# Transposes of normalised tokens and attention outputs: from TensorE to the DMA engines

## The chip, the cores and the metric

The kernel runs on one core of a Trainium2 chip. The metric is the device time of one execution in microseconds (us), lower is better. The engines are PE (TensorE), DVE (VectorE), ACT (ScalarE), POOL (GpSimd) and SP (SyncE, which here only issues DMAs). In the traces PE's results lie in PSUM (`ps_all`), from where DVE or ACT copy them to the working memory, SBUF.

## The reference

Two layers, each of them attention followed by a gated MLP, on 2048 tokens of width 512, in bfloat16:

```python
def _A_ref(x, wq, wk, wv, wo):             # 32 heads of 16, one shared key and value
    q = heads(x @ wq); k = x @ wk; v = x @ wv
    p = softmax(einsum('bhqd,bkd->bhqk', q, k) * 16 ** -0.5)
    return merge(einsum('bhqk,bkd->bhqd', p, v)) @ wo

def _B_ref(x, w_in, w_sp, b_sp, w_out):    # F = 1792, halves of 896
    z = gelu(x @ w_in)
    z1, z2 = z[..., :896], layernorm(z[..., 896:])
    g = einsum('ts,bsf->btf', w_sp, z2) + b_sp[None, :, None]
    return (z1 * g) @ w_out

x = x + A(layernorm(x)); x = x + B(layernorm(x))     # layer 0
x = x + A(layernorm(x)); x = x + B(layernorm(x))     # layer 1, same weights
```

There are 32 heads x 2048 x 2048 exponentials per layer. A *block* below is 128 keys x 512 columns of scores; there are 4096 blocks in all.

## The kernel before

The kernel is written by a list scheduler in Python. Every operation has an engine, an assumed duration, dependencies and a priority; the scheduler plays them against a model of the core and emits one fixed instruction order per engine, with semaphore waits. So any edit of a duration in the model gives another order of the same work.

The exponential of a block is computed in one of two ways. ACT takes groups of two or three blocks with one `ACTIVATE`. DVE takes a pair of blocks now and then, with a polynomial of seven instructions. The scheduler decides block by block:

```python
    def take(self, t, js):                 # may DVE take a block, at time t?
        if sc.bank_free() > t:             # needs one of the two side banks of PSUM
            return None
        ...
            backlog = sc.free["dve"] - t + sum(o.dur for o in sc.ready["dve"] if ...)
            if backlog > BACKLOG:
                return None
```

Layer norm of token tiles (128 tokens x 512), then four PE transposes per tile into a side bank, and a copy out of PSUM by DVE, or by ACT if it has a gap:

```python
        def pe(e, b):
            ins = None
            for i, sl in enumerate(slots):
                for kd in range(KD):
                    k = i * KD + kd
                    ins = e.transpose(self.b16(b)[:, k * 128:(k + 1) * 128],
                                      self.xn[:, sl, kd * 128:(kd + 1) * 128], self.ident[:])
            return ins
        ...
        pt, (ev,) = sc.job([(pe, n * 4 * 0.06)], [dict(
            fn=lambda e, b: e.tensor_copy(*cp(b)), dur=d_psum(n * 256), prio=pr, deps=dst_deps,
            alts=[("act", lambda e, b: e.activation(*cp(b), ACTF.Copy), d_act(n * 512) + 0.1)])], ...)
```

`ln` serves the keys of a layer (destination `xnTA`) and the MLP's input (`xnTB`). `project` does the same for the attention output `on`, into `onT`, before the multiplication with `wo`. Tokens come in chunks of 512, 512, 512, 256, 128 and 128; the work of one chunk's MLP runs beside the next chunk's attention. When the last chunk's attention is over, a serial chain finishes the layer, and the second layer's keys can start.

The softmax here doesn't subtract the row's maximum and nothing guards it: scores larger than these inputs give would overflow.

Of the kernel before, what the change touches and what calls it, by code (L numbers as in the profile page):

```python
# [57 lines left out]
class Sched:  # L58
# [3 lines left out]
    def __init__(self, side_banks):  # L62
        self.free = {e: 0.0 for e in ENGS}
        self.ready = {e: [] for e in ENGS}
        self.streams = {e: [] for e in ENGS}
        self.order = {e: [] for e in ENGS}
        self.commits = []
        self.banks = [Bank(b) for b in side_banks]
        self.seq = 0
        self.table = "exp"  # L70
        self.cache = {}
        self.nleft = 0
        self.exp_next = None
        self.tick = {}
        self.hist = []
        self.lent = {}
        self.dma_free = 0.0

    def lend(self, key, idxs, o):
# [139 lines left out]
    def commit(self, o, t, eng=None):  # L219
        eng = eng or o.eng  # L220
        if eng != o.eng:
            for e, f, d in o.alts:
                if e == eng:
                    o.fn, o.dur = f, d
        if o.ready is not None:
            if o in self.ready[o.eng]:
                self.ready[o.eng].remove(o)
                self.cache.pop(o.eng, None)
            for e, _f, _d in o.alts:
                if o in self.ready[e]:  # L230
                    self.ready[e].remove(o)
                    self.cache.pop(e, None)
        o.eng = eng
        if o.first:
            b = min([b for b in self.banks if not b.busy and not b.closed], key=lambda b: b.free_at)
            b.busy = True
            o.job.bank = b
            o.deps += [d for d in b.rel if d not in o.deps]
        o.start = t
        dur = o.dur  # L240
        if eng == "pe":
            k = int(t / TICK)
            if not self.fast(t):
                dur = o.slow
            self.hist.append((t + dur, o.cols))
            k = int((t + dur) / TICK)
            self.tick[k] = self.tick.get(k, 0.0) + o.cols
        if o.table is not None and o.table != self.table:
            self.table = o.table
            dur += 1.3  # L250
        o.end = t + dur
        o.vis = o.end + (LAT[eng] if o.lat is None else o.lat)
        if o.dma:
            self.dma_free = max(self.dma_free, o.end) + o.dma / 240e3
            o.vis = self.dma_free + 1.9
        self.free[eng] = o.end
        self.order[eng].append(o)
        self.commits.append(o)
        self.nleft -= 1
        if o.job is not None and o in o.job.last:  # L260
            o.job.left -= 1
            if o.job.left == 0:
                b = o.job.bank
                b.busy = False
                b.rel = list(o.job.last)
                b.free_at = max(x.vis for x in o.job.last)
        self.cache.pop(eng, None)
        for u in o.users:
            u.nun -= 1
            if u.nun == 0:  # L270
                self._arm(u)
        if o.at_commit is not None:
            o.at_commit(o)
        return o
# [106 lines left out]
def d_act(n):  # L381
    return n * 0.8333e-3 + 0.06

# [22 lines left out]
class Kern:  # L406
    def __init__(self, nc, A_x, A_wq, A_wk, A_wv, A_wo, B_x, B_w_in, B_w_sp, B_b_sp, B_w_out, out):
# [42 lines left out]
        self.xn = sb([P, 4, D], BF16, "xn")  # L450
        self.xnTA = sb([P, KD, S], BF16, "xnTA")
        self.xnTB = sb([P, KD, 512], BF16, "xnTB")
        self.qs = sb([P, NQS, 512], BF16, "qs")
# [11 lines left out]
        self.on = sb([P, 4, D], BF16, "on")  # L465
        self.onT = sb([P, 4, 512], BF16, "onT")
        self.rden = sb([P, 2, 4, 4], FP32, "rden")
# [55 lines left out]
    def b16(self, b):  # L523
        return self.ps16[:, 1024 * b:1024 * (b + 1)]

    def dma(self, fn, deps, sem, nbytes, prio=5.0, eng="sp", issue=0.5):
# [77 lines left out]

    def ln(self, tiles, deps_t, dst, dst_deps, pr, urgent=False):
        sc = self.sc
# [15 lines left out]
        for t in tiles:  # L622
# [5 lines left out]
                op1=ALU.mult), 0.22, [r, self.last_xn[sl]], pr + 0.3))  # L628

        def pe(e, b):  # L630
            ins = None
# [7 lines left out]
        def cp(b):  # L639
            return (dst.rearrange("p kd (t c) -> p t kd c", c=128),  # L640
                    self.b16(b)[:, 0:n * 512].rearrange("p (t kd c) -> p t kd c", t=n, kd=KD))
        pt, (ev,) = sc.job([(pe, n * 4 * 0.06)], [dict(
            fn=lambda e, b: e.tensor_copy(*cp(b)), dur=d_psum(n * 256), prio=pr, deps=dst_deps,  # L643
            alts=[("act", lambda e, b: e.activation(*cp(b), ACTF.Copy), d_act(n * 512) + 0.1)])], xo + [self.c_id], pr)
        for sl in slots:
            self.last_xn[sl] = pt
        return ev


    def layer_keys(self, layer):  # L650
        sc = self.sc
        for p in range(8):
            def build(p=p):
# [4 lines left out]
                for tt in ([ts[:1], ts[1:]] if p < 2 else [ts]):  # L658
                    evs.append(self.ln(tt, lambda t: [self.x_op[t]],
                                       self.xnTA[:, :, tt[0] * 128:(tt[-1] + 1) * 128], dd, pr, p < 2))  # L660
                self.xnTA_read[p] = []

                def kpe(e, b):
                    ins = None
                    for kd in range(KD):
                        ins = e.matmul(self.b32(b)[:, 0:256], self.wk_rep[:, kd, :], self.xnTA[:, kd, p * 256:(p + 1) * 256],
                                       start=(kd == 0), stop=(kd == KD - 1))
                    return ins

                def vpe(e, b):  # L670
                    ins = None
                    for i, t in enumerate(ts):
                        for kd in range(KD):
                            ins = e.matmul(self.b32(b)[:, 256 + 128 * i:384 + 128 * i],
                                           self.xnTA[:, kd, t * 128:(t + 1) * 128], self.wv_rep[:, kd, :],
                                           start=(kd == 0), stop=(kd == KD - 1))
# [79 lines left out]
    def make_q(self, q, war=()):  # L756
# [4 lines left out]
        def pe(e, b, h):  # L761
            ins = None
            for i in range(g.nh):
                for kd in ((0, 1), (2, 3))[h] if g.nh == 1 else range(4):
                    if g.nh == 1 or i // (g.nh // 2) == h:
                        ins = e.matmul(self.b32(b)[:, i * n:(i + 1) * n], self.wq_pad[:, kd, g.hg + i, :],  # L766
                                       self.xnTA[:, kd, g.t0:g.t0 + n], start=(kd == 0), stop=(kd == KD - 1))
            return ins
# [63 lines left out]
    def project(self, g, norms):  # L832
# [7 lines left out]
        for h in range((nq + 1) // 2):  # L840
# [11 lines left out]
            def cp(b, qts=qts):  # L852
                m = len(qts)
                return (self.onT[:, :, qts[0] * 128:(qts[0] + m) * 128].rearrange("p c (qt q) -> p c qt q", q=128),
                        self.b16(b)[:, 0:m * 512].rearrange("p (qt c q) -> p c qt q", qt=m, c=4))
            m = len(qts)
            pl, (ev,) = sc.job([(pe, m * 4 * 0.06)], [dict(
                fn=lambda e, b, cp=cp: e.tensor_copy(*cp(b)), dur=d_psum(m * 256), prio=0.7, deps=list(self.onT_read),
# [6 lines left out]
        for qt in range(nq):  # L865
            t = g.t0 // 128 + qt

            def pe(e, b, qt=qt):
                ins = None
                for c in range(4):  # L870
                    ins = e.matmul(self.b32(b)[:, 0:D], self.onT[:, c, qt * 128:(qt + 1) * 128], self.wo_r[:, c, :],
                                   start=(c == 0), stop=(c == 3))
                return ins
            pl, (xo,) = sc.job([(pe, 4 * d_mm(512))], [dict(
                fn=lambda e, b, t=t: e.tensor_tensor(self.X[:, t, :], self.b32(b)[:, 0:D], self.X[:, t, :], ALU.add),
                dur=d_psum(512), prio=0.8, deps=[self.x_op[t]])], [evs[qt // 2], self.l_wo], 1.4)
            self.onT_read.append(pl)
# [4 lines left out]
    def mixer_chunk(self, g):  # L882
# [8 lines left out]
        for i in range(0, nt, 2):  # L891
            ts = T[i:i + 2]
            evs.append(self.ln(ts, lambda t: [self.x_op[t]], self.xnTB[:, :, i * 128:(i + len(ts)) * 128], war, pr, last))
        self.xnTB_read = []
        z2 = []
        z1 = []
        for i, t in enumerate(T):
            for h in range(2):
                def pe(e, b, ks, i=i, h=h):
                    ins = None  # L900
                    for kd in ks:
                        ins = e.matmul(self.b32(b)[:, 0:448], self.xnTB[:, kd, i * 128:(i + 1) * 128],  # L902
                                       self.w_in_r[:, kd, FH + h * 448:FH + (h + 1) * 448], start=(kd == 0),
# [3 lines left out]
                def cp(b, t=t, h=h):  # L907
# [8 lines left out]
                                                d_act(448) + 0.1)])],  # L916
                                   [evs[i // 2], self.l_win], pr + 0.2)
                z2.append(ev)
# [12 lines left out]
        for f0 in range(0, NF, per):  # L931
# [3 lines left out]
            def pe(e, b, part, f0=f0):  # L935
                ins = None
                for (f, kd) in part:
                    ins = e.matmul(self.b32(b)[:, (f - f0) * n:(f - f0 + 1) * n], self.w_in_r[:, kd, f * 128:(f + 1) * 128],  # L938
                                   self.xnTB[:, kd, 0:n], start=(kd == 0), stop=(kd == KD - 1))
                return ins  # L940
# [33 lines left out]
        else:  # L974
            gs = z1 = [sc.op("act", gl, d_act(NF * nt * 128) + d_act(nt * FH), z1 + z2, -1.0, table="gelu")] * (2 * nt)
        for (zt, zn, v) in zs:
# [116 lines left out]
    def closing(self, layer):  # L1093
# [9 lines left out]
        for tc in range(8):  # L1103
# [43 lines left out]
            for tt in range(2):  # L1147
                t = tc * 2 + tt

                def pe(e, b, ks, tt=tt, par=par):  # L1150
# [8 lines left out]
                    dur=d_psum(512), prio=0.8, deps=[self.x_op[t]])], [self.l_wout], pr - 0.3,  # L1159
                    piece_deps=[hs[0:1], hs[1:2], hs[2:4]], soft=evs)  # L1160
                self.hT_read[par].append(pl)
# [482 lines left out]
```

## Time and profile before

| | before |
|---|---|
| median of all runs (us) | 1877.7 when predicted, 1878.4 with one run more |
| span of the profiled run | 1873.8 us |
| busy: ACT, DVE, PE | 1764.5, 1745.3, 1609.1 us |
| blocks by ACT, by DVE | 3599, 497 |
| attention of layer 0 ends, of layer 1 ends | 885.78, 1819.05 us |

The page gives the busy time and share of the span for each engine:

```profile
span 1873.8 us, 30967 instructions
PE 1609.1 (86%) x12242; PEld 498.9 (27%) x12242; DVE 1745.3 (93%) x3131; ACT 1764.5 (94%) x1580; POOL 53.4 (3%) x94
```

The view by windows tells stretches apart. Columns: start and end, length, then busy us and instructions of PE, PEld (weight loads), DVE, ACT and POOL, then the granted PE clock, the share of busy DMA engines and GB/s:

```profile
100.00:200.00 100.00, 79.66 (x634) 20.81 (x632) 98.63 (x166) 100.00 (x89) 0.00 (x0) 1.00 0.00 1
...
600.00:750.00 150.00, 135.91 (x1042) 42.15 (x1044) 139.45 (x247) 148.05 (x126) 3.77 (x6) 0.99 0.09 28
...
880.00:1000.00 120.00, 102.02 (x759) 44.04 (x755) 98.84 (x224) 82.97 (x105) 9.49 (x18) 1.00 0.12 35
```

In pure attention ACT is at 100% and DVE at 98.6%, PE at 80%. With an MLP beside it, ACT is at 98.7%, DVE at 93%, PE at 91%. At the end of a layer ACT falls to 69%.

The groups of instructions that matter, from the costliest-groups view. Columns: line, engine, operation, output and input, shapes, count, then busy us and mean ns of one, then the idle time just before and what ended it:

```profile
L1319 ACT ACTIVATE Pa<-ps_all 128x1536 bf16<-128x1536 f32 (+1 forms) x1440 | 1643.1, 1355 | 29.4 <-PE ps_all L1591 21.7
L1496 DVE TENSOR_SCALAR E<-ps_all 128x512 int32<-128x512 f32 x497 | 338.5, 683 | 28.7 <-PE ps_all L1591 27.3
L635 PE MATMUL ps_all<-ident,xn 128*128 128x128 bf16 x256 | 20.7, 220 | 9.7 <-DVE xn L626 5.3 <-DVE E L1496 2.5 <-DVE E L1131 0.8
L848 PE MATMUL ps_all<-ident,on 128*128 128x128 bf16 x128 | 10.2, 220 | 0.5 <-DVE on L812 0.3
L858 DVE COPY onT<-ps_all 128x1024 bf16<-128x1024 bf16 x14 | 9.5, 683 | 0.1
L643 DVE COPY xnTB<-ps_all 128x1024 bf16<-128x1024 bf16 x13 | 8.9, 683 | 0.2 <-PE ps_all L635 0.2
```

The first two are the exponentials (DVE's is only the first of its seven instructions). The other four are what the change removes, all but the last chunk's and the keys that stay (below).

Not all of PE's busy time is work. Where the scheduler's model has seen few matmul columns in the last 3.4 us, it puts in a matmul on a tile of zeros that nothing reads (the kernel calls these *warm*):

```profile
L1577 PE MATMUL ps_all<-zero 128*128 128x512 bf16 x882 | 272.3, 391 | 4.8 <-DVE gp L1076 2.6 <-POOL zero L574 1.0 <-DVE E L1496 0.8
```

Of the 80 us of PE in 100 to 200 us they are 28 us, of the 136 us in 600 to 750 us they are 9 us. So PE's 86% overstates how full it is.

### The profile page before, as it was taken

How to read it: one execution, taken by the hardware profiler on the slowest of the kernel's cores; microseconds unless marked ns; L12 is line 12 of the kernel's file. 1: busy time of each engine (PE TensorE's matmuls, PEld its weight loads, DVE VectorE, ACT ScalarE, POOL GpSimd, SP SyncE). 2: the span in 40 equal slices, each digit the busy share in tenths (PEclk: the TensorE clock that was granted, in tenths of full speed). 3: DMA queues.
4: the chain of work that ended last, by engine and by line, in shares of the span. 5: the costliest groups of instructions: out<-in, count | busy, mean ns of one | idle time of the engine just before them, and what ended most of it. 6: DMA issues, size and time to landing. Idle time of an engine off the chain costs nothing.

```text
span 1873.8 us, 30967 instructions
## 1 busy us (share of the span) xinstructions
PE 1609.1 (86%) x12242; PEld 498.9 (27%) x12242; DVE 1745.3 (93%) x3131; ACT 1764.5 (94%) x1580; POOL 53.4 (3%) x94
## 2 busy tenths in 40 slices
PE   8877888888799998988888778888888799999898
PEld 3222222222222232322432222222222222323234
DVE  8999999999799899997879999999999799989978
ACT  8999999999999999998579999999999999999983
POOL 2000000000000000000100000000000000000000
PEclk9999999999899999998999999999999899999999
DMA  9800000000101001021110000000000100010113
GB/s 275 215 1 1 1 1 1 1 1 1 40 1 46 23 1 43 13 66 45 55 33 1 1 1 1 1 1 1 1 1 1 40 23 24 24 43 24 55 45 109
DMA packets 85976, 59.17 MB, mean 32 GB/s; under 512 B 40004, under 2 KB 82248, under 8 KB 85832
## 3 DMA queue, kind: packets, MB, share of 16 engines
q1 hardware_dynamic: 84248, 57.03, 10.6%
q8 instruction: 97, 1.59, 0.4%
q14 instruction: 47, 0.39, 0.1%
q10 hardware_dynamic: 1584, 0.16, 0.1%
HBM read 30.97 MB, written 17.83 MB: 26 GB/s over the span
## 4 chain that ended last, share of the span: by engine, by line
ACT 33%; DVE 28%; PE 25%; issue 13%; POOL 1%; ACTq 0%; POOLq 0%
ACT Pa L1319 31%; PE ps_all L1064 7%; PE ps_all L1591 6%; DVE E L1496 5%; PE ps_all L1395 4%; DVE Pd L1534 3%; DVE E L1529 2%; DVE E L1532 2%; DVE E L1523 2%; PE ps_all L1153 2%; DVE st L611 2%; PE ps_all L938 1%; PE ps_all L902 1%; DVE E L1526 1%; DVE E L1525 1%
## 5 line engine op out<-in xcount | busy, mean ns | idle before, releaser
L1319 ACT ACTIVATE Pa<-ps_all 128x1536 bf16<-128x1536 f32 (+1 forms) x1440 | 1643.1, 1355 | 29.4 <-PE ps_all L1591 21.7
L1591 PE MATMUL ps_all<-qs,kT 32*128 32x512 bf16 x4096 | 564.0, 387 | 215.7 <-ACT Pa L1319 201.2
L1496 DVE TENSOR_SCALAR E<-ps_all 128x512 int32<-128x512 f32 x497 | 338.5, 683 | 28.7 <-PE ps_all L1591 27.3
L1591 PEld LDWEIGHTS ps_all<-qs,kT 32*128 32x128 bf16 x4096 | 139.0, 91 | 758.9 <-ACT Pa L1319 683.5
L1395 PE MATMUL ps_all<-Pa,V 128*32 128x512 bf16 x3599 | 320.7, 387 | 0.0
L1534 DVE SCALAR_TENSOR_TENSOR Pd<-E 128x1024 uint16<-128x1024 int32 (+1 forms) x249 | 301.9, 1212 | 0.5
L1577 PE MATMUL ps_all<-zero 128*128 128x512 bf16 x882 | 272.3, 391 | 4.8 <-DVE gp L1076 2.6
L1064 PE MATMUL ps_all<-wsT,z2n 128*128 128x512 bf16 x714 | 195.4, 382 | 5.3 <-DVE z2n L999 2.2
L1395 PE MATMUL ps_all<-Pd,V 128*32 128x512 bf16 x497 | 172.4, 387 | 0.0
L1529 DVE TENSOR_TENSOR E<-E 128x1024 f16<-128x1024 f16 (+1 forms) x249 | 169.7, 682 | 2.8
L1532 DVE TENSOR_TENSOR E<-E 128x1024 f16<-128x1024 f16 (+1 forms) x249 | 169.9, 682 | 2.1
L1523 DVE TENSOR_SCALAR E<-E 128x1024 f16<-128x1024 uint16 (+1 forms) x249 | 169.9, 682 | 1.3
L1526 DVE TENSOR_SCALAR E<-E 128x1024 f16<-128x1024 f16 (+1 forms) x249 | 104.1, 418 | 2.3
L1525 DVE TENSOR_SCALAR E<-E 128x1024 f16<-128x1024 f16 (+1 forms) x249 | 104.2, 419 | 2.0
L1577 PEld LDWEIGHTS ps_all<-zero 128*128 128x128 bf16 x882 | 67.3, 98 | 144.6 <-issue 109.1
L1395 PEld LDWEIGHTS ps_all<-Pa,V 128*32 128x32 bf16 x3599 | 63.8, 94 | 117.4 <-issue 110.7
L1076 DVE TENSOR_TENSOR gp<-ps_all,gp 128x512 f16<-128x512 f32 x112 | 75.1, 684 | 20.0 <-PE ps_all L1064 19.7
L1064 PEld LDWEIGHTS ps_all<-wsT,z2n 128*128 128x128 bf16 x714 | 55.0, 97 | 100.3 <-issue 49.5
L766 PE MATMUL ps_all<-xnTA,wq_pad 128*128 128x512 bf16 (+2 forms) x384 | 69.6, 313 | 1.5 <-DVE X L1158 0.6
L902 PE MATMUL ps_all<-w_in_r,xnTB 128*128 128x448 bf16 x256 | 62.9, 355 | 3.6 <-DVE xnTB L643 1.7
L938 PE MATMUL ps_all<-xnTB,w_in_r 128*128 128x512 bf16 (+2 forms) x336 | 60.4, 310 | 2.2 <-DVE z1s L949 0.9
L989 DVE BATCH_NORM_STATS2 st<-z2n 128x6 f32<-128x448 bf16 x64 | 36.3, 600 | 22.4 <-ACT z2n L970 16.7
(89 smaller groups left out, 1098.9 us busy)
## 6 DMA issues: line engine op xcount, KB each, us to landing
wsT_scratch<-gp SPq DMA_DIRECT2D x16, 512.0 KB, 3.7
wsT<-wsT_scratch SPq DMA_DIRECT2D x8, 1024.0 KB, 5.5
z1s<-z_scratch SPq DMA_DIRECT2D x16, 448.0 KB, 3.8
wsT<-wsT_scratch SPq DMA_DIRECT2D x8, 512.0 KB, 3.6
z_scratch<-z1s SPq DMA_DIRECT2D x4, 896.0 KB, 5.6
X<-in_A_x_dram SPq DMA_DIRECT2D x8, 256.0 KB, 5.6
out_dram<-X SPq DMA_DIRECT2D x16, 128.0 KB, 2.0
w_in_r<-in_B_w_in_dram SPq DMA_DIRECT2D x1, 1792.0 KB, 10.3
```

The costliest lines, as they stand in the source:

```text
L1064: ins = e.matmul(self.b32(b), self.z2n[:, s, f * 128:(f + 1) * 128], w_[:, s - s0, :], start=st, stop=sp)
L1319: return e.activation(k.Pa[:, base:base + n, :], k.b32(b0, n).rearrange("p (k q) -> p k q", k=n), ACTF.Exp, scale=SCALE)
L1395: ins = e.matmul(k.b32(k.pvb)[32 * j:32 * j + 32, :], k.V[:, u.kt, 32 * j:32 * j + 32], b.slot, tile_position=(0, 32 * j), start=u.first, ...
L1496: return k.sc.op("dve", lambda e: e.tensor_scalar(k.eI[:, s, 512 * i:512 * (i + 1)], k.b32(j.bank.idx)[:, 0:512], C_LOG2, C_BIAS, op0=ALU. ...
L1523: return lambda e: e.tensor_scalar(out, a, m, None, op0=ALU.mult)
L1525: return lambda e: e.tensor_scalar(out, a, b, None, op0=ALU.add)
L1526: return lambda e: e.tensor_scalar(out, a, m, b, op0=ALU.mult, op1=ALU.add)
L1529: o4 = sc.op("dve", lambda e: e.tensor_tensor(q, u, w, ALU.mult), d_sb(n, 0.521e-3), [o3], pr)
L1532: o6 = sc.op("dve", lambda e: e.tensor_tensor(q, q, u, ALU.mult), d_sb(n, 0.521e-3), [o5], pr)
L1534: o7 = sc.op("dve", lambda e: e.scalar_tensor_tensor(po.bitcast(U16), I, 2.0 ** -9, q, op0=ALU.mult, op1=ALU.add), d_sb(n, 1.042e-3), [o6] ...
L1577: return e.matmul(k.b32(k.pvb if b is None else b.idx), k.zero[:], k.zero[:, None, :].to_broadcast([P, 4, P]), start=b is not None, stop=b ...
L1591: return e.matmul(self.b32(bank), self.kT[32 * j:32 * j + 32, kt * 128:(kt + 1) * 128], self.qs[32 * j:32 * j + 32, g.q.slot, :], tile_pos ...
```

## The change

The intent is to take 288 PE transposes and the 38 copies out of PSUM behind them off the three compute engines, for 72 of the 96 token tiles, and let the DMA engines transpose from SBUF to SBUF. A *handoff* below is the way of a finished tile through its transpose to the first matmul that reads it. The last chunk (where every handoff is waited for), the first two pairs of keys and all keys of layer 0 stay on PE. The rest of the diff edits the scheduler's model. The core of it:

```diff
+    def transpose(self, out, src, deps, sem, pr):
+        return self.dma(lambda e: e.dma_start_transpose(out, src), deps, sem, 131072, pr, issue=1.25)
@@ ln
+        if not urgent and not on_pe:
+            evs = []
+            for i, (t, sl) in enumerate(zip(tiles, slots)):
+                o = self.transpose(dst[:, i, :, :], self.xn[:, sl, :], [xo[i]] + dst_deps, f"xt{sl}", pr)
+                self.last_xn[sl] = o
+                evs.append(o)
+            return evs
@@ project
+            if g.ci < len(self.chunks) - 1:
+                for qt in qts:
+                    o = self.transpose(self.onT[:, qt, :, :], self.on[:, qt, :], norms + list(self.onT_read), f"ot{qt}", 0.7)
+                    ...
+                continue
@@ tiles laid out so that each tile's transpose is contiguous
-        self.xnTA = sb([P, KD, S], BF16, "xnTA")
+        self.xnTA = sb([P, self.NT, KD, 128], BF16, "xnTA")
         ... (xnTB and onT likewise, and the matmuls that read them)
@@ the scheduler's model
 def d_act(n):
-    return n * 0.8333e-3 + 0.06
+    return n * 0.8333e-3 + 0.051
+def d_gelu(n):                                   # used for the large gelus
+    return n * 0.86e-3 + 0.1
+            if o.sem == "fill" and self.full:     # score matmuls after side work
+                dur += 0.09
+            self.full = o.sem not in ("fill", "pv")
-                    piece_deps=[hs[0:1], hs[1:2], hs[2:4]], soft=evs)
+                    piece_deps=[hs[0:1], hs[1:2], hs[2:4]], soft=evs + [self.gp_ops[(tg, f)] for f in range(NF)])
```

All DMA transposes are issued from SP, one stream. The Trainium skill ("DMA: Bandwidth & Descriptors", Rules for kernel authors) says that two streams which both transpose must be serialised, or can corrupt each other silently.

More of the change, by code (lines that the diff above doesn't have):

```diff
@@ L77, in __init__ @@
         self.dma_free = 0.0
+        self.full = False
     def lend(self, key, idxs, o):
@@ L450, in __init__ @@
         self.xn = sb([P, 4, D], BF16, "xn")
-        self.xnTA = sb([P, KD, S], BF16, "xnTA")
-        self.xnTB = sb([P, KD, 512], BF16, "xnTB")
+        self.xnTA = sb([P, self.NT, KD, 128], BF16, "xnTA")
+        self.xnTB = sb([P, 4, KD, 128], BF16, "xnTB")
         self.qs = sb([P, NQS, 512], BF16, "qs")
@@ L465, in __init__ @@
         self.on = sb([P, 4, D], BF16, "on")
-        self.onT = sb([P, 4, 512], BF16, "onT")
+        self.onT = sb([P, 4, 4, 128], BF16, "onT")
         self.rden = sb([P, 2, 4, 4], FP32, "rden")
@@ L602, in load, with ln @@
         self.c_v = pm(self.V[:].rearrange("p t (c r) -> p t c r", r=32)[:, :, :, DH], 1.0, 64, 0.8, [m])
-    def ln(self, tiles, deps_t, dst, dst_deps, pr, urgent=False):
+    def ln(self, tiles, deps_t, dst, dst_deps, pr, urgent=False, on_pe=False):
         sc = self.sc
@@ L639, in cp @@
         def cp(b):
-            return (dst.rearrange("p kd (t c) -> p t kd c", c=128),
-                    self.b16(b)[:, 0:n * 512].rearrange("p (t kd c) -> p t kd c", t=n, kd=KD))
+            return dst, self.b16(b)[:, 0:n * 512].rearrange("p (t kd c) -> p t kd c", t=n, kd=KD)
         pt, (ev,) = sc.job([(pe, n * 4 * 0.06)], [dict(
@@ L646, in ln @@
             self.last_xn[sl] = pt
-        return ev
+        return [ev]
     def layer_keys(self, layer):
@@ L658, in build @@
                 for tt in ([ts[:1], ts[1:]] if p < 2 else [ts]):
-                    evs.append(self.ln(tt, lambda t: [self.x_op[t]],
-                                       self.xnTA[:, :, tt[0] * 128:(tt[-1] + 1) * 128], dd, pr, p < 2))
+                    evs += self.ln(tt, lambda t: [self.x_op[t]], self.xnTA[:, tt[0]:tt[-1] + 1, :, :], dd, pr, p < 2,
+                                   layer == 0)
                 self.xnTA_read[p] = []
@@ L665, in kpe @@
                     for kd in range(KD):
-                        ins = e.matmul(self.b32(b)[:, 0:256], self.wk_rep[:, kd, :], self.xnTA[:, kd, p * 256:(p + 1) * 256],
+                        ins = e.matmul(self.b32(b)[:, 0:256], self.wk_rep[:, kd, :], self.xnTA[:, 2 * p:2 * p + 2, kd, :],
                                        start=(kd == 0), stop=(kd == KD - 1))
@@ L674, in vpe @@
                             ins = e.matmul(self.b32(b)[:, 256 + 128 * i:384 + 128 * i],
-                                           self.xnTA[:, kd, t * 128:(t + 1) * 128], self.wv_rep[:, kd, :],
+                                           self.xnTA[:, t, kd, :], self.wv_rep[:, kd, :],
                                            start=(kd == 0), stop=(kd == KD - 1))
@@ L766, in pe @@
                         ins = e.matmul(self.b32(b)[:, i * n:(i + 1) * n], self.wq_pad[:, kd, g.hg + i, :],
-                                       self.xnTA[:, kd, g.t0:g.t0 + n], start=(kd == 0), stop=(kd == KD - 1))
+                                       self.xnTA[:, g.t0 // 128:(g.t0 + n) // 128, kd, :], start=(kd == 0), stop=(kd == KD - 1))
             return ins
@@ L853, in cp @@
                 m = len(qts)
-                return (self.onT[:, :, qts[0] * 128:(qts[0] + m) * 128].rearrange("p c (qt q) -> p c qt q", q=128),
-                        self.b16(b)[:, 0:m * 512].rearrange("p (qt c q) -> p c qt q", qt=m, c=4))
+                return (self.onT[:, qts[0]:qts[0] + m, :, :],
+                        self.b16(b)[:, 0:m * 512].rearrange("p (qt c q) -> p qt c q", qt=m, c=4))
             m = len(qts)
+            if g.ci < len(self.chunks) - 1:
+                for qt in qts:
+                    o = self.transpose(self.onT[:, qt, :, :], self.on[:, qt, :], norms + list(self.onT_read), f"ot{qt}", 0.7)
+                    self.on_read[qt] = [o]
+                    evs.append(o)
+                continue
             pl, (ev,) = sc.job([(pe, m * 4 * 0.06)], [dict(
@@ L870, in pe @@
                 for c in range(4):
-                    ins = e.matmul(self.b32(b)[:, 0:D], self.onT[:, c, qt * 128:(qt + 1) * 128], self.wo_r[:, c, :],
+                    ins = e.matmul(self.b32(b)[:, 0:D], self.onT[:, qt, c, :], self.wo_r[:, c, :],
                                    start=(c == 0), stop=(c == 3))
@@ L875, in project @@
                 fn=lambda e, b, t=t: e.tensor_tensor(self.X[:, t, :], self.b32(b)[:, 0:D], self.X[:, t, :], ALU.add),
-                dur=d_psum(512), prio=0.8, deps=[self.x_op[t]])], [evs[qt // 2], self.l_wo], 1.4)
+                dur=d_psum(512), prio=0.8, deps=[self.x_op[t]])], [evs[qt], self.l_wo], 1.4)
             self.onT_read.append(pl)
@@ L892, in mixer_chunk @@
             ts = T[i:i + 2]
-            evs.append(self.ln(ts, lambda t: [self.x_op[t]], self.xnTB[:, :, i * 128:(i + len(ts)) * 128], war, pr, last))
+            evs += self.ln(ts, lambda t: [self.x_op[t]], self.xnTB[:, i:i + len(ts), :, :], war, pr, last)
         self.xnTB_read = []
@@ L901, in pe @@
                     for kd in ks:
-                        ins = e.matmul(self.b32(b)[:, 0:448], self.xnTB[:, kd, i * 128:(i + 1) * 128],
+                        ins = e.matmul(self.b32(b)[:, 0:448], self.xnTB[:, i, kd, :],
                                        self.w_in_r[:, kd, FH + h * 448:FH + (h + 1) * 448], start=(kd == 0),
@@ L916, in mixer_chunk @@
                                                 d_act(448) + 0.1)])],
-                                   [evs[i // 2], self.l_win], pr + 0.2)
+                                   [evs[i], self.l_win], pr + 0.2)
                 z2.append(ev)
@@ L938, in pe @@
                     ins = e.matmul(self.b32(b)[:, (f - f0) * n:(f - f0 + 1) * n], self.w_in_r[:, kd, f * 128:(f + 1) * 128],
-                                   self.xnTB[:, kd, 0:n], start=(kd == 0), stop=(kd == KD - 1))
+                                   self.xnTB[:, 0:n // 128, kd, :], start=(kd == 0), stop=(kd == KD - 1))
                 return ins
@@ L974, in mixer_chunk @@
         else:
-            gs = z1 = [sc.op("act", gl, d_act(NF * nt * 128) + d_act(nt * FH), z1 + z2, -1.0, table="gelu")] * (2 * nt)
+            gs = z1 = [sc.op("act", gl, d_gelu(NF * nt * 128) + d_gelu(nt * FH), z1 + z2, -1.0, table="gelu")] * (2 * nt)
         for (zt, zn, v) in zs:
```

## The prediction

> **What bounds the kernel now.** The table of busy time by engine has ACT 1764.5 us (94%), DVE 1745.3 us (93%), PE 1609.1 us (86%) of a 1873.8 us span. Softmax blocks go to ACT or DVE as the schedule finds room. In stretches of pure attention (windows, 100:200 and 1000:1100 us) ACT is at 100%, DVE at 98.5%, PE at 80%: two engines share the load and both are full. In stretches with mixer work beside attention (500:700) ACT is at 98%, DVE 93%, PE 93%. Idle time of ACT, 109 us in all, sits mostly at 850:1000 (40 us) and 1800:1874 (37 us), where one layer ends in a serial chain of the last chunk. The chain of waits is 33% ACT, 28% DVE, 25% PE.
>
> **What the change removes.** 72 token tiles (30 attention outputs, 30 mixer inputs, 12 keys of layer 1) lose four PE transposes each and their PSUM eviction. By the groups of instructions: on DVE 14 onT and 13 xnTB copies of 128x1024 (683 ns), four xnTA copies of the second layer, and four 128x512 copies (414 ns): 22.8 us. On ACT two xnTA and one xnTB copy (1.02 us): 3.1 us. On PE 288 transposes, 0.080 us of busy time each (10.2 us for 128): 23 us. A PSUM bank of the two side banks is free 38 times more.
>
> **What it adds.** 72 SBUF to SBUF DMA transposes of 128x512 on SP. The trace's own DMA transposes (2048x128, 16 blocks) take 2.86 us of SP's queue and 5.0 us from issue to landing; scaled to four blocks I estimate about 1 us of SP and 2.5 to 3 us to landing, 70 us of a queue that mostly waits. The path through PE takes about 1.5 to 2 us, so each handoff gets 1 to 1.5 us longer. The Trainium skill ("VectorE: DVE Perf Modes", The three transpose paths) also has the DMA path slower for one 128x128 block, 1309 against 390 ns; no run here shows that yet. Mixer tiles and out-projections have tens of us of attention to hide in. Only the second layer's keys (920:975), where ACT starves, can show the latency: at most 2 us once, for the last pair. The last chunk, the serial one, is left as it is.
>
> **What it is worth.** DVE time is bought back at a poor rate. One softmax block costs DVE 2.73 us (the E and Pd groups over 497 blocks) and ACT 0.457 us (1643.1 over 3599). With both full, 22.8 us of DVE and 3.1 us of ACT free (22.8 + 3.1 x 5.98)/(1 + 5.98) = 5.9 us of span. The other edits are of the scheduler's model (fill dearer after side work, gelu dearer, exp cheaper, projections held until the gate sums are scheduled). They aim at ACT's 22 us of waits for scores and DVE's 17 us of waits for gelu; I give them 4 us, uncertain in sign. Together about 10 us: 1868 us, 0.5% faster. Range 1850 to 1882. Faster by over 2% 0.03, within 2% 0.95, slower 0.02.
>
> **What would show it.** DVE softmax blocks up from 497 by 5 to 15; copies into onT, xnTB, xnTA down by 38; landing of the new DMAs under 4 us; ACT still 100% in pure attention; the idle stretches near 900 and 1830 us unchanged.
>
> **What would make it wrong.** Transposes that land in 5 us or more, or queue on SP behind loads of 512 KB and 1 MB; a static order, made by a model, that goes wrong at the layer boundary, where every engine then waits in line; or PE having been the true limit in the mixer stretches, which would make 23 us of PE worth more.

One number in it was read from the wrong window: 98, 93 and 93% fit 520 to 720 us (98.5, 93.6 and 93.4%); for 500 to 700 us the view by windows has ACT 97.7%, DVE 90.0% and PE 89.6%. The argument did not rest on it.

## More of the kernel before

The timeline of ACT where layer 0 ends (start, duration, instruction, and in brackets the idle time before it):

```profile
885.78 1.28 ACT L1335 ACT_TABLE_LOAD   x1
890.78 0.60 ACT L859 ACTIVATE onT<-ps_all 128x512 bf16<-128x512 bf16 x1 [3.51 <-PE ps_all L848]
897.71 0.60 ACT L644 ACTIVATE xnTB<-ps_all 128x512 bf16<-128x512 bf16 x1 [6.33 <-PE ps_all L635]
904.00 1.28 ACT L973 ACT_TABLE_LOAD   x1
```

From the first table load (attention is over) to the second are 18.2 us of one chain, in which ACT mostly waits. Its two copies there are the last chunk's handoffs.

## The result, and the profile after

| | before | after |
|---|---|---|
| median (us) | 1878.4 (4 runs) | 1869.5 (4 runs, 1868.2 to 1871.4) |
| ratio | | 0.9954, interval 0.9940 to 0.9968 |
| busy: ACT, DVE, PE | 1764.5, 1745.3, 1609.1 | 1756.6, 1736.9, 1595.0 |
| blocks by ACT, by DVE | 3599, 497 | 3595, 501 |
| attention ends, layer 0 and 1 | 885.78, 1819.05 | 880.47, 1812.60 |

A ratio is the mean time of one kernel's runs over the mean of the other's runs of the same rounds, so not quite the ratio of the two medians. 0.0046 of 1878 us is 8.6 us. The change is faster, clear of noise, but by less than 2%.

```profile
span 1867.6 us, 30386 instructions
PE 1595.0 (85%) x11889; PEld 477.3 (26%) x11889; DVE 1736.9 (93%) x3107; ACT 1756.6 (94%) x1581; POOL 53.4 (3%) x94
```

The windows, and the groups that answer to those of before:

```profile
100.00:200.00 100.00, 79.20 (x624) 19.97 (x620) 97.60 (x164) 99.16 (x89) 0.00 (x0) 0.98 0.00 1
...
600.00:750.00 150.00, 136.63 (x1032) 40.84 (x1031) 144.76 (x250) 147.93 (x127) 2.38 (x4) 1.00 0.10 25
...
880.00:1000.00 120.00, 99.85 (x725) 41.03 (x727) 106.70 (x238) 83.08 (x105) 9.32 (x18) 1.00 0.17 39
```

```profile
L1343 ACT ACTIVATE Pa<-ps_all 128x1536 bf16<-128x1536 f32 (+1 forms) x1439 | 1637.5, 1368 | 31.1 <-PE ps_all L1615 16.2
L1520 DVE TENSOR_SCALAR E<-ps_all 128x512 int32<-128x512 f32 x501 | 341.1, 683 | 28.8 <-PE ps_all L1615 26.3
L1601 PE MATMUL ps_all<-zero 128*128 128x512 bf16 x817 | 263.3, 393 | 2.1 <-POOL zero L585 1.0 <-DVE X L1182 0.8 <-DVE gp L1100 0.2
L654 PE MATMUL ps_all<-ident,xn 128*128 128x128 bf16 x88 | 7.5, 220 | 5.6 <-DVE xn L637 5.4
L866 PE MATMUL ps_all<-ident,on 128*128 128x128 bf16 x8 | 0.8, 219 | 0.0
```

The PE transposes of tokens and outputs fell from 384 to 96, and no DVE copy into `onT` or `xnTB` is left. The new DMAs, from the view of DMA issues (count, median us from issue to landing), and SP's part from the view of one tile (min, median and max ns):

```profile
onT<-on SPq DMA_TRANSPOSE x30, 2.5
xnTB<-xn SPq DMA_TRANSPOSE x30, 2.4
xnTA<-xn SPq DMA_TRANSPOSE x12, 2.5
```

```profile
L535 SPq DMA_TRANSPOSE onT<-on x30: 1189/1267/2308, 224.6 to 1758.2; - x30
```

One tile costs SP 1.2 to 1.27 us (medians) and lands after 2.4 to 2.5 us, at worst 4.2 us in any of the three groups. The end of layer 0:

```profile
880.47 1.28 ACT L1359 ACT_TABLE_LOAD   x1
884.35 0.60 ACT L883 ACTIVATE onT<-ps_all 128x512 bf16<-128x512 bf16 x1 [2.39 <-PE ps_all L866]
891.51 0.60 ACT L662 ACTIVATE xnTB<-ps_all 128x512 bf16<-128x512 bf16 x1 [6.56 <-PE ps_all L654]
897.80 1.28 ACT L997 ACT_TABLE_LOAD   x1
```

It starts 5.3 us earlier and is as long as before (17.3 us). The two profiled runs differ by 6.2 us (1873.8 and 1867.6), not by 8.6. Taking them apart by ACT's windows: the attention of layer 0 became 5.3 us shorter, of which 1.9 us is less ACT work (862.6 to 860.7) and 3.4 us less waiting (23.1 to 19.7). From there to the end of the second attention only 1.1 us was gained: 5.9 us less ACT work (883.5 to 877.6), but 4.8 us more waiting (49.8 to 54.6). The rest, 55 us, did not change. So over four fifths of these 6.2 us lie in layer 0, although the second layer has more of the change in it.

### The profile page after: what moved, and what is told of

Its sections match the earlier page's. It is cut to its first block, busy times and chain, and to the rows that moved or that the text cites. A ratio compares the mean times of both kernels' runs of the same rounds, so it can differ in the third digit from the quotient of the medians.

```text
span 1867.6 us, 30386 instructions
## 1 busy us (share of the span) xinstructions
PE 1595.0 (85%) x11889; PEld 477.3 (26%) x11889; DVE 1736.9 (93%) x3107; ACT 1756.6 (94%) x1581; POOL 53.4 (3%) x94
## 4 chain that ended last, share of the span: by engine, by line
ACT 36%; DVE 30%; PE 18%; issue 14%; POOL 1%; ACTq 0%; POOLq 0%; DVEq 0%
ACT Pa L1343 34%; PE ps_all L1088 6%; PE ps_all L1615 5%; DVE E L1520 5%; DVE Pd L1558 4%; PE ps_all L1419 3%; DVE E L1556 2%; DVE E L1553 2%; DVE E L1547 2%; DVE gp L1100 2%; PE ps_all L1177 1%; DVE st L622 1%; DVE E L1550 1%; DVE E L1549 1%; DVE z2n L937 1%
## 5 line engine op out<-in xcount | busy, mean ns | idle before, releaser
L1419 PE MATMUL ps_all<-Pa,V 128*32 128x512 bf16 x3595 | 324.9, 388 | 1.5 <-DVE Pd L1558 0.6
L1558 DVE SCALAR_TENSOR_TENSOR Pd<-E 128x1024 uint16<-128x1024 int32 x251 | 304.4, 1213 | 1.1
L1601 PE MATMUL ps_all<-zero 128*128 128x512 bf16 x817 | 263.3, 393 | 2.1 <-POOL zero L585 1.0
L1419 PE MATMUL ps_all<-Pd,V 128*32 128x512 bf16 x501 | 177.7, 389 | 0.0
L1553 DVE TENSOR_TENSOR E<-E 128x1024 f16<-128x1024 f16 x251 | 171.3, 682 | 3.4
L1556 DVE TENSOR_TENSOR E<-E 128x1024 f16<-128x1024 f16 x251 | 171.0, 681 | 2.5
L1547 DVE TENSOR_SCALAR E<-E 128x1024 f16<-128x1024 uint16 x251 | 171.1, 682 | 1.6
L1549 DVE TENSOR_SCALAR E<-E 128x1024 f16<-128x1024 f16 x251 | 104.5, 416 | 2.2
L1550 DVE TENSOR_SCALAR E<-E 128x1024 f16<-128x1024 f16 x251 | 104.3, 415 | 2.3
L1601 PEld LDWEIGHTS ps_all<-zero 128*128 128x128 bf16 x817 | 62.7, 98 | 138.0 <-issue 116.8
L1177 PE MATMUL ps_all<-E 128*128 128x512 bf16 x224 | 53.6, 380 | 4.2 <-ACT E L1156 3.6
```

Of the source, the lines that this page charges most:

```text
L1419: ins = e.matmul(k.b32(k.pvb)[32 * j:32 * j + 32, :], k.V[:, u.kt, 32 * j:32 * j + 32], b.slot, tile_position=(0, 32 * j), start=u.first, ...
L1547: return lambda e: e.tensor_scalar(out, a, m, None, op0=ALU.mult)
L1549: return lambda e: e.tensor_scalar(out, a, b, None, op0=ALU.add)
L1550: return lambda e: e.tensor_scalar(out, a, m, b, op0=ALU.mult, op1=ALU.add)
L1553: o4 = sc.op("dve", lambda e: e.tensor_tensor(q, u, w, ALU.mult), d_sb(n, 0.521e-3), [o3], pr)
L1556: o6 = sc.op("dve", lambda e: e.tensor_tensor(q, q, u, ALU.mult), d_sb(n, 0.521e-3), [o5], pr)
```

## The experiments

**Theory A** is the prediction's: freed DVE and ACT time is bought back by moving blocks from ACT to DVE, so ACT time counts 6/7 and DVE time 1/7, PE time nothing. **Rival B**: the model edits made the gain. **Rival C**: PE limited the stretches with MLP work, so its 23 us counted. A fourth possibility came up only with the results: **D**, the gain is the luck of another order. A fifth, **E**, the granted clock of PE, was tested by no run; what the record shows of it stands after e10.

| run | ratio to before | interval | us against before | us against the changed kernel |
|---|---|---|---|---|
| changed kernel | 0.9954 | 0.9940 to 0.9968 | -8.6 | 0 |
| e1_dma_only | 0.9955 | 0.9942 to 0.9967 | -8.4 | +0.2 |
| e2_model_only | 1.0029 | 1.0017 to 1.0041 | +5.4 | +14 |
| e3_keys_pe | 0.9961 | 0.9949 to 0.9973 | -7.3 | +1.3 |
| e4_last_dma | 0.9988 | 0.9976 to 1.0000 | -2.3 | +6.4 |
| e5_dve_back | 0.9982 | 0.9966 to 0.9998 | -3.4 | +5.3 |
| e6_act_load | 1.0061 | 1.0042 to 1.0080 | +11.5 | +20 |
| e7_pe_back | 0.9978 | 0.9964 to 0.9992 | -4.1 | +4.5 |
| e8_twice | 1.0053 | 1.0041 to 1.0065 | +10.0 | +19 |
| e9_nudge_before | 0.9946 | 0.9934 to 0.9959 | -10.1 | -1.5 |
| e10_nudge_after | 0.9964 | 0.9950 to 0.9977 | -6.8 | +1.9 |
| e11_pe_double | 1.0069 | 1.0057 to 1.0081 | +13.0 | +22 |
| e12_ot_dma | 1.0018 | 1.0003 to 1.0033 | +3.4 | +12 |

The last column is the difference of two ratios, times 1878 us. The changed kernel was timed in other rounds than the rest, so such a difference carries the errors of both: 3.5 to 4.4 us. Every run gave correct results.

### e1 and e2: each half of the change alone

```diff
e1 (from the changed kernel): the model as before
-    return n * 0.8333e-3 + 0.051
+    return n * 0.8333e-3 + 0.06
-                dur += 0.09
+                dur += 0.0
  (d_gelu back to d_act, and soft=evs)

e2 (from the changed kernel): no DMA transposes
-        if not urgent and not on_pe:
+        if False:
-            if g.ci < len(self.chunks) - 1:
+            if False:
```

> The DMA transposes as in the changed kernel, but the four edits of the scheduler's model undone. Theory A (the gain is freed DVE and ACT time, bought back by moving softmax blocks from ACT to DVE): 504 DVE blocks by construction against 497, about 6 us below the kernel before, ratio 0.997. Rival B (the gain is the scheduler's better model, the transposes give nothing): within 2 us of before. Rival C (PE was the limit in the mixer stretches): 8 us or more below, with ACT's idle time next to score matmuls falling in 400:850 us.

> The four edits of the scheduler's model alone, all transposes on PE as before. 494 DVE blocks by construction. Theory A: 2 to 4 us below before (ratio 0.998 to 0.999), the sum with the DMA-only run being about the whole 8.6 us. Rival B: the whole gain, 8 us below (0.9955).

With the transposes alone the kernel was 8.4 us faster; with the model edits alone it was 5.4 us slower, and on top of the transposes they gave nothing. That speaks against rival B, as far as one order for each can (see e9). The DVE blocks behaved as theory A says: 504 against 497 with the transposes alone, 494 with the model edits alone, 501 with both. Each time the transposes added seven. But -8.4 and +5.4 do not add up to -8.6; the two halves interact through the order.

### e3: the second layer's keys back on PE

```diff
-                    evs += self.ln(tt, ..., dd, pr, p < 2, layer == 0)
+                    evs += self.ln(tt, ..., dd, pr, p < 2, True)
```

> The changed kernel with the second layer's 12 key tiles back on PE. Theory A: those six jobs are worth 2.7 us of DVE and 2 us of ACT, but at the boundary the DMA's 1 us longer handoff is exposed, so within 2 us of the changed kernel either way (ratio to before 0.9945 to 0.9965). If the boundary's latency had cost more than that, this run would be 3 us or more faster than the changed kernel.

1.3 us slower than the changed kernel, with overlapping intervals. No difference is seen, as expected; that the DMA's longer handoff and the saved copies cancel at the layer's boundary is not shown separately.

### e4: the last chunk by DMA too

```diff
-            if g.ci < len(self.chunks) - 1:
+            if True:
-            evs += self.ln(ts, ..., war, pr, last)
+            evs += self.ln(ts, ..., war, pr, last, by_dma=True)     # overrides "urgent"
```

> The changed kernel with the last chunk's transposes by DMA as well (the exception lifted; keys as in the change). Theory A: the last chunk is a serial chain in both layers, two handoffs each; a DMA handoff is about 2.5 us to landing plus wait, against about 1.2 us by PE and ACT, so 1 to 1.5 us times four: 4 to 6 us slower than the changed kernel, half of it before the attention of the second layer starts and half after 1812 us. If latency were hidden everywhere, no difference.

6.4 us slower. The timeline of ACT has the same two table loads at the end of layer 0:

```profile
881.90 1.28 ACT L1360 ACT_TABLE_LOAD   x1
902.48 1.28 ACT L998 ACT_TABLE_LOAD   x1
```

They are 20.6 us apart against 17.3 us in the changed kernel, and in layer 1 21.9 against 18.3 us: 3.3 and 3.6 us for two handoffs each, 1.7 us per handoff. The two make 6.9 us, the whole difference within its error. This length alone would not prove it, for the same chain lasts 16.1 to 18.8 us in the other kernels. But the steps show it too. From the normalised output `on` to the first matmul with `wo`, at the end of layer 0, in the changed kernel and in e4:

```profile
883.44 0.41 DVE L830 TENSOR_TENSOR on<-ps_all,rden 128x256 bf16<-128x256 bf16 x1
885.23 1.03 PE L895 MATMUL ps_all<-wo_r,onT 128*128 128x512 bf16 x4
```

```profile
884.87 0.41 DVE L830 TENSOR_TENSOR on<-ps_all,rden 128x256 bf16<-128x256 bf16 x1
889.03 1.03 PE L895 MATMUL ps_all<-wo_r,onT 128*128 128x512 bf16 x4
```

From the end of the one to the start of the other are 1.38 us against 3.75 us, in layer 1 1.95 against 3.88 us. From the normalised tokens to the first matmul of the MLP they are 1.15 and 1.14 us against 2.47 and 2.49 us. Together e4's four handoffs took 7.0 us longer, 1.3 to 2.4 us each. This is the cleanest result: where a handoff is waited for, DMA costs 1.7 us more on average than PE and a copy, and the exception in the change is right.

### e5, e6, e7: give back the time of one engine

```python
# dead work at each of the places where a PSUM copy went away; nothing reads the result
e5: sc.op("dve", bn_stats(scr[:, 0:6], wq_pad[:, 0, 0:4, :]), 0.6, deps, prio=0.4)              # 38 of them
e6: sc.op("act", activation(scr, wk_rep[:, 0:2, :], Copy), d_act(256) + 0.1, deps, prio=-0.5)   # 72, one per tile
e7: sc.job([4n transposes of wk_rep into a side bank], [tensor_copy of one column, 0.09])       # 38 jobs, 288 transposes
```

> The changed kernel, with one dead DVE instruction of about 0.67 us (statistics of a constant tile, read by nothing) at each of the 38 places where a PSUM copy went away: 25 us of DVE time back, no dependency, no PE, no PSUM bank. Theory A: DVE time is worth 1/7, so 3 to 4 us slower than the changed kernel. If DVE and ACT limited the kernel equally, and DVE time counted in full, 12 us or more slower. Rival C (PE): no change.

> The changed kernel, with 72 dead ACT instructions of about 0.39 us (copies of a constant 128x256 tile) at the same places: 28 us of ACT time, about as much as the DVE run adds on DVE. Theory A: ACT time is worth 6/7, so 20 to 26 us slower than the changed kernel, some six times the DVE run's effect. If ACT had slack where the mixer runs, under 12 us.

> The changed kernel, with 288 dead PE transposes of a constant tile at the places where the real ones went away, each group in a side PSUM bank that a dead DVE copy of one column gives free again (38 such copies, about 0.1 us each). Theory A: PE time replaces warming matmuls, so within 2 us of the changed kernel. Rival C: PE was the limit in the mixer stretches, so most of the 8.6 us comes back.

The dead instructions, from the traces (e5 in the groups, with its exponentials on DVE, e6 in the timeline, e7 in the groups):

```profile
L1530 DVE TENSOR_SCALAR E<-ps_all 128x512 int32<-128x512 f32 x501 | 340.9, 684 | 33.2 <-PE ps_all L1625 30.8
L673 DVE BATCH_NORM_STATS2 scr<-wq_pad 128x6 f32<-128x512 bf16 x38 | 26.1, 687 | 0.0
```

```profile
273.28 0.41 ACT L674 ACTIVATE scr<-wk_rep 128x256 bf16<-128x256 bf16 x1
273.58 1.02 ACT L1355 ACTIVATE Pa<-ps_all 128x1024 bf16<-128x1024 f32 x1
```

```profile
L676 PE MATMUL ps_all<-ident,wk_rep 128*128 128x128 bf16 x288 | 22.7, 221 | 3.7 <-DVE gp L1116 1.1 <-DVE xn L638 1.0 <-DVE z2n L953 0.8
```

e6 needs a correction of my own arithmetic: an ACT instruction overlaps the next one. The dead copy shown lasts 0.41 us (the mean of the 72 is 0.53), but the exponential after it starts 0.30 us later, so 72 of them hold ACT for about 22 us, not 28; ACT's busy time rose by 20.7 us. They cost 20 us: about theory A's 6/7. e5 put 26 us on DVE and cost 5.3 us (3 to 4 were expected, 26 would be full price). Per microsecond, as measured, ACT's time (20 / 22) cost four to five times DVE's (5.3 / 26).

But theory A's mechanism did not act in these runs. By it, 26 us more on DVE should push about 8 blocks back to ACT, and 22 us more on ACT about 7 blocks over to DVE (both over 2.73 + 0.457 us a block). e5 kept 501 DVE blocks, as in the changed kernel, and e6 has 503. Nor is e5's loss spread like a price: in the profiled runs its attention of layer 0 ends 14.6 us later than the changed kernel's (895.11 against 880.47 us), and the stretch from there to the end of the second attention is 6.1 us shorter (926.0 against 932.1). So 5.3 us is one order's result, with an error of 4 us, and not a measured price of DVE's time.

e7 put 23 us on PE, with 6 us of small DVE copies, and cost 4.5 us where theory A allowed 2. The scheduler took part of PE's load back: there are 784 matmuls on zeros in place of 817, 10 us less. Taken alone this would say that PE's relief made half of the gain. The next runs say how far such a number can be trusted.

### e9 and e10: how much is the luck of an order?

```diff
-LAT = {"pe": 0.22, "act": 0.22, "dve": 0.14, "pool": 0.12, "sp": 0.0}
+LAT = {"pe": 0.22, "act": 0.22, "dve": 0.145, "pool": 0.12, "sp": 0.0}
```

> The kernel before, with one number of the scheduler's model changed that stands for nothing here (the time until another engine sees a DVE result, 0.140 to 0.145 us): the same instructions in another order. It measures how much time is only the luck of an order. If differences of a few us are meaningful, within 2 us of before; if orders scatter by as much as the change gained, 5 us or more away on either side.

> The changed kernel with the same meaningless nudge (496 DVE blocks by construction against 501). If the gain belongs to the transposes and not to the order, it stays at least 5 us below both the kernel before and the nudged kernel before; if orders scatter by as much, the two nudged kernels may tie.

This result puts the others in their place. Five nanoseconds in the model's idea of when a DVE result becomes visible, which stand for nothing, made the kernel *before* 10.1 us faster, with every transpose still on PE. That is as much as the whole change gained. The same nudge on the changed kernel cost 1.9 us, within the error. So the two nudged kernels stand at 0.9946 and 0.9964, with overlapping intervals: the change, seen from there, is worth nothing, or even costs 3 us.

The page of the nudged kernel before:

```profile
span 1867.5 us, 30782 instructions
PE 1595.2 (85%) x12087; PEld 498.6 (27%) x12223; DVE 1747.1 (94%) x3132; ACT 1762.5 (94%) x1579; POOL 52.1 (3%) x94
```

DVE still does its copies (1747 us, against 1737 in the changed kernel), ACT was hardly relieved (1762.5 against 1764.5), and yet the span is that of the changed kernel. And the nudged changed kernel has only 496 DVE blocks, fewer than before, without being slow. So the number of blocks does not tell the time to within 10 us; idle time that comes and goes with the order does.

What can be said over all orders that were tried: the four kernels with the transposes in the change's places or nearly so and nothing else added (changed, e1, e3, e10) lie at -8.6, -8.4, -7.3 and -6.8 us; the three with all transposes on PE (before, e2, e9) at 0, +5.4 and -10.1 us. The means are -7.8 and -1.6 us, a difference of 6.2 us, close to the 5.9 us that was costed. But with three orders on one side that differ by 15 us among themselves, this does not settle it.

**E, the granted clock, is a rival that no run tested.** Executions of one and the same kernel differ in the mean granted clock of PE, and their time goes with it. Of e10's six, the fastest took 1867.65 us at a clock of 0.990, the slowest 1876.51 us at 0.981. Fitted within each kernel over 104 executions, the time is 1.0 us longer for each 0.001 of clock lost (correlation -0.92). The kernels differ in it as well: on average 0.986 before, 0.990 changed, 0.988 in e1 and e9, 0.984 in e4 and e5, 0.980 in e6, 0.977 in e12. If the same slope held between kernels, it would account for about 4 of the change's 8.6 us, for all of the 5.3 us of e5 and the 12 us of e12, for half of the 20 us of e6, and for 2 of e9's 10 us. These are estimates, and no correction: the clock may itself follow from the order, and in e4, where the clock would account for most of the loss, the traced handoffs already do.

### e8 and e11: doubled latency and doubled PE time

```diff
e8: each transpose twice, the second waiting for the first
+                o = self.transpose(dst[:, i, :, :], self.xn[:, sl, :], [o], f"xt{sl}", pr)
e11: e7 with every dead transpose issued twice
-            for k in range(4 * n):
+            for k in [*range(4 * n)] * 2:
```

> The changed kernel with every one of the 72 DMA transposes done twice, the second waiting for the first: 1.25 us more of SP and about 2.5 us more until the consumer may go, per tile. Theory A: handoffs in attention stretches have tens of us of slack, only the second layer's keys show it: 0 to 3 us slower. If latency was what kept the gain small, 5 us or more slower.

> As the run with 288 dead transposes on PE, but with 576. The same 38 banks and small copies, twice the PE time. If PE time caused that run's 4 to 5 us, this one loses 8 to 10 us against the changed kernel (ratio to before above 1.0); if it was the banks and small copies, or the luck of an order, it stays within 3 us of that run (ratio 0.996 to 0.9995).

Both lost about 20 us, far more than expected, and both lost most of it in one place: between 870 and 1000 us ACT is idle for 65 and 59 us, against 37 us in the changed kernel. The waits of ACT there, first in the changed kernel, then in e8, then in e11 (total us, times, longest):

```profile
ACT kT L705 <- PE ps_all L692: 8.3, 5, 4.5
```

```profile
ACT kT L706 <- PE ps_all L693: 31.5, 6, 21.6
```

```profile
ACT kT L720 <- PE ps_all L707: 27.2, 5, 21.3
```

ACT waits over 21 us for one pair of the second layer's keys. The DVE timelines show why. The last addition of a gate sum (`gp`, the `w_sp` product) of layer 0, in the changed kernel, in e8 and in e11:

```profile
890.93 1.28 DVE L1100 TENSOR_TENSOR gp<-ps_all,gp 128x512 f16<-128x512 f32 x2
```

```profile
967.70 1.28 DVE L1102 TENSOR_TENSOR gp<-ps_all,gp 128x512 f16<-128x512 f32 x2
```

```profile
976.60 0.68 DVE L1116 TENSOR_TENSOR gp<-ps_all,gp 128x512 f16<-128x512 f32 x1
```

In e1 to e5, e7, e9 and e10 the last gate sum is done between 888 and 907 us, beside the last chunk's chain. In e8 five and in e11 seven additions were left over and stand in the middle of the second layer's start. The last tokens' output, their layer norm and their keys wait for them, and in e8's chain of waits the run of work goes through exactly these steps from 963 to 984 us. That the leftovers are the cause is read from the traces; I made no run that only moves them. So e8 as a whole does not measure latency and e11 as a whole does not measure PE time: each tipped the scheduler's order over an edge. e11 had also lost 7.1 us before that (its attention of layer 0 ends at 887.60 us against 880.47 us, in e7 at 877.86 us); whether that is PE time or the order stays open. In the attention of layer 0, doubled latency cost next to nothing (it ends at 881.45 us against 880.47 us).

### e12: one step further

```diff
+        if g.ci < len(self.chunks) - 1:
+            tp = self.transpose(self.oN[:], self.oT[:, par, :], [ev] + self.oN_read, "oN", 0.6)
+            m = sc.op("dve", reciprocal of self.oN's denominators, 0.22, [tp, self.rd_read[par]], 0.6)
+            ... (normalisation from self.oN in SBUF instead of PSUM)
-        self.xn = sb([P, 4, D], BF16, "xn")
+        self.xn = sb([P, 3, D], BF16, "xn")           # to make room
```

> A step further: the transposes of the unnormalised attention outputs (60 groups, 240 transposes on PE, 60 uses of a side bank) also by DMA, except in the last chunk, with the reciprocal and the normalisation then read from SBUF; the second layer's keys back on PE, and three slots for normalised tokens in place of four, to make room. 507 DVE blocks by construction. Theory A with DVE, PE and side banks all worth something: 3 to 8 us below the changed kernel, about 1864 us. If the longer chain per group (about 1.3 us) is exposed, slower than the changed kernel.

The second layer's keys go back to PE. The kernel was 12 us slower than the changed one, in spite of 507 DVE blocks and 192 PE transposes fewer (240 of `oT` less, 48 of the keys more). Two things stand out in its trace. Its last gate sum is at 917.9 us, later than in any of the undisturbed runs. And SP's DMAs stand in the order of issue: after 22 us the `w_sp` loads come in groups, each behind a transpose of `oT` that waited for its attention group (at 50, 75, 98 us and on), so that their last one is issued at 179 us instead of 72 us. The mean granted PE clock of the profiled run was 0.972, the lowest of all. Which of these costs how much was not separated. The step is not worth taking in this form, and no version was found that clearly beats the changed kernel; e9 ties with it.

## Why the prediction was right, point by point

The time was right: 1868 us foretold, 1869.5 us measured. The way to it was right in parts, and that its parts caused the gain is not shown.

- **What bounds the kernel.** Right for ACT as far as e6 goes: 22 us more of its time cost 20 us, where a nudge of the order was seen to do 10; the granted clock may have a share in it. That DVE's time counts 1/7 is not shown: e5's 5.3 us is no more than an order can do, and no block moved back.
- **What is removed and added.** Right: 38 copies and 288 transposes went, 72 DMA transposes came. SP's share was set at about 1 us and measured at 1.2 to 1.27 us; landing at 2.5 to 3 us, measured 2.4 to 2.5 us.
- **The idle stretches.** Right: in pure attention ACT stayed at 99 to 100%, and the chain at the end of layer 0 takes 17.3 us against 18.2, that of layer 1 18.3 against 18.2.
- **Latency.** Right where the change uses it (e3: the keys make no difference; e4: the 1.7 us per handoff that the exception avoids).
- **Blocks moved to DVE.** 5 to 15 more were foretold, 4 came, just short of the range. ACT's busy time fell by 7.9 us; the 3.1 us of copies and four blocks (1.8 us) make 4.9 us of it. With the transposes alone it is seven, and the costing implies (5.9 - 3.1) / 0.457 = 6. The model edits took three back. The check was set on the wrong quantity all the same: e10 shows a fast kernel with 496 blocks.
- **The worth of the transposes, 5.9 us.** Not refuted, not shown. Alone they gave 8.4 us (e1), over the orders tried 6.2 us on average, and from one nudged kernel to the other the whole change cost 3.4 us.
- **The model edits, 4 us "uncertain in sign".** Wrong as a term of the sum: they gave 0 us on top of the transposes and cost 5.4 us alone. A term of -8.6 us was costed as -5.9 and -4.
- **PE time worth nothing.** Open. e7 lost 4.5 us, which is within what an order can do; e11 was spoiled in the second layer, and the 7.1 us that it lost in layer 0 would fit rival C as well as an order.
- **What was missing.** The prediction names a static order that goes wrong at the layer boundary as a risk, but has no term for the scatter of orders in general. With e9 in hand, an honest estimate would have been -6 us from the transposes, plus or minus some 8 us from the order. The granted clock is missing too. That the result fell within 2 us of the middle is in part luck.

## What to carry to other kernels

When an instruction order comes from a scheduler, first measure what a meaningless nudge of its model does; here it was worth 10 us of 1878, more than most edits that one would want to judge, and a single pair of orders cannot credit a gain of half a per cent to its intended cause. Moving small transposes to the DMA engines showed no cost where consumers are far off (in e8, with the latency doubled, the attention of layer 0 ended 1 us later) and cost 1.7 us per handoff where they were waited for, so an exception for the serial tail is worth its lines. To price an engine's time, add dead work to it, but under several orders and with the granted clock beside each time: here 20 odd microseconds cost 20 us on ACT and 5 us on DVE, and only the first is larger than the 15 us that lie between two orders of the same work (e2 and e9).

## What the Trainium skill lacked or had wrong

- "VectorE: DVE Perf Modes", The three transpose paths, gives 1309 ns for one 128x128 block by DMA and 390 ns by PE. The runs add what a kernel needs: four such blocks in one SBUF to SBUF transpose take SP 1.2 to 1.27 us and land 2.4 to 2.5 us after issue (at worst 4.2 us), so the time is not four times that of one. A PE transpose of one block lasted 0.22 us here.
- "TensorE: Matmul & The Clock Gate", Part 4: PE-mode transpose, says that the output goes to PSUM and needs a DVE copy after. The trace agrees, with 683 ns per 128x1024 copy on DVE; ACT did some of the copies here (1.02 us for 128x1024). It has no comparison of the whole handoff; in e4 the DMA's was 1.7 us longer on average.
- None of the pages that I read on reading traces warns that the order of the same instructions alone moves the time; here by 10 us in 1878 (e9).
